# Routing attention with a tanh-shrink block: four pairs turned on TensorE, and the similarities turned and routed in PSUM between the fill's products

## The chip, the cores and the metric

The kernel runs on one core of one Trainium2 chip. A core has TensorE (matrix products, written to PSUM), VectorE, ScalarE and GpSimd (called DVE, ACT and POOL in the profile), the SyncE queue (SP) that issues most transfers here, and 16 DMA engines. The metric is device time in microseconds (us) of the whole program, the median of its runs; lower is better. The profile is of one further execution of the same program. A difference under 0.3% is about what the runs of this kernel can't tell from no difference.

## The reference

The program is attention in which a query attends only to the keys of its own cluster, followed by a two-layer block. `q`, `k` and `v` have 4 batches, 8 heads, 768 positions and 64 dimensions; each head has 16 centroids.

```python
q_assign = np.argmax(np.einsum('bhsd,hcd->bhsc', q_n, c_n), axis=-1)
k_assign = np.argmax(np.einsum('bhsd,hcd->bhsc', k_n, c_n), axis=-1)
mask = q_assign[:, :, :, None] == k_assign[:, :, None, :]
scores = scale * np.matmul(q, k.transpose(0, 1, 3, 2))
scores = np.where(mask, scores, -1000000000.0)
...
attn = np.exp(scores)
attn = attn / (np.sum(attn, axis=-1, keepdims=True) + 1e-09)
return np.matmul(attn, v).astype(np.float32)
...
h = x @ w_in
g = h - np.tanh(h)
return (g @ w_out).astype(np.float32)
```

`q_n`, `k_n` and `c_n` are the rows divided by their norms. Between the two parts the heads are put side by side, so `x` has 3072 rows of 512; `w_in` is 512 by 2048 and `w_out` 2048 by 512.

## The kernel before, in words

**Pairs and steps.** Two heads of one batch make a pair; there are 16, four a batch (`HP = 4`, `pairs` numbered 0 to 15). A pair's queries come in two halves of 384 columns, and its keys in three groups of two blocks of 128 (`NS = 3`). One *step* is a pair, a half and a group of keys: `steps` lists 96 of them. The first 12 (`HALF`) take pairs 0 to 3 with their first halves, the next 12 the same pairs' second halves, and from step 24 on each pair has six steps in a row (pair 4 has steps 24 to 29, and so on). In a step TensorE makes the scores of the *following* step (`begin`, L481), ScalarE their exponential (L503), VectorE multiplies it by the mask, which compares the codes of queries and keys (`select`, L513), and TensorE multiplies the step's own masked weights by `v` (`value`, L536). In the first halves of pairs 1 to 3 the mask is added to the scores on TensorE instead (L492), from one-hot codes (`hot`, prepared by VectorE in `one_hot`, L456 and L460, after a transfer that spreads the codes), and the sums of the weights are a product too (L551).

**The fill.** From step 12 on TensorE also computes the second block for the batch whose attention is finished. Its products are cut into items, and the loop over steps takes as many as its share of the work. Steps 12 to 23 do up-products L710 and down-products L726 of batch 0's first half; steps 24 to 47 the second half; from step 48 on each batch has 24 steps of seven-product (Strassen) items, first 56 short ones (L913, evacuated by L908 on VectorE and L918 on ScalarE, with the tanh L980 or L967), then 21 long ones (L1009). The last batch's come after the last step. A product takes a bank from the PSUM pool `ps_f`, which has three; the similarities, the codes on their way out (`pq`) and the denominators share them. The scores live in `ps_s`, two tiles of two banks.

**Where other work goes.** The order on every engine is the order in which the program issues. Each step collects a list `todo`: the two masks of the following step, the stages of pairs to come, sums, weights to be rounded, checks. `between`, which every product calls after its matmuls (most after their evacuation), spreads the list evenly over the step's products. In steps 24 to 35 the masks are taken ahead of the first product.

**From a pair to its codes.** `load` brings `q` and `k`, `turn` puts head dimensions on partitions, `similar` makes the products with the centroids (L376, 16 small ones on one `ps_f` bank), `turn_back` puts positions on partitions again (L386), `route` finds the largest of 16 (L394) and marks it (L396), `route_on` multiplies the marks by 16, 15, ..., 1 (L405) and takes the largest as the code (L407), `publish` turns the codes (L423) and sends them to DRAM (`q_codes`, L429). From there `spread` and `spread_both` bring them back to all partitions as `row` and `hot`.

Pairs 0 and 1 (`rowwise`) are loaded by rows, one transfer a head (L332), turned by six TensorE transposes into a `ps_s` tile (L355) and copied out by ScalarE or VectorE (L362, L364). All others are loaded as 32 by 32 blocks, two transfers a head (L340), and turned by one VectorE transpose per operand (L348). In the prologue, pairs 0 and 1 are taken through all stages by hand.

The dictionary `ready` places the stages of the other pairs. For pairs 2 and 3 the first step is 3 * (n - 2): turns at 0, `similar` at 1, `route` and `route_on` at 1, `publish` and the spreading at 2, `one_hot` at 4. For pairs 4 to 15 it is step 18 (pair 4) or the first step of the pair before: turns one step earlier, `similar` at 0, `route` at 1, `publish` at 3. A stage with two parts puts its second under `BEHIND + i`. In the loop over steps, stage 1 (`similar`) is taken ahead of `begin`, and where the step has a stage 1 and is past the first 12, `value` goes before both (`values_first`). `turn_back` then is the first entry of `todo`, ahead of the masks.

Of the kernel before, what the change touches and what calls it, by code (L numbers as in the profile page):

```python
# [30 lines left out]
F32 = mybir.dt.float32  # L31
# [8 lines left out]
P = 128  # L40
# [18 lines left out]
def kernel(  # L59
# [119 lines left out]
    def fast():  # L179
# [133 lines left out]
        def rowwise(n: int):  # L313

            return n < 2
# [66 lines left out]
        def turn_back(n: int):  # L382

            ps = sims[n]
            t = sims[n] = rtp.tile([P, TB], F32, name="simt")
            nc.vector.transpose(out=t, in_=ps.rearrange("p i j t -> p (i j t)"))  # L386

        def route(n: int):

            G = HCH * 8  # L390
            pr = sims.pop(n).rearrange("p (g c) -> p g c", c=C)
            shape = [P, G, C]
            mx = rtp.tile([P, G], F32, name="mx")
            nc.vector.reduce_max(out=mx, in_=pr, axis=AX.X)  # L394
            top = tops[n] = rtp.tile(shape, F32, name="top")
            nc.vector.tensor_tensor(  # L396
                out=top, in0=pr, in1=mx.unsqueeze(2).to_broadcast(shape), op=ALU.is_ge
            )
# [3 lines left out]
        def route_on(n: int):  # L402
            top = tops.pop(n)
            places = down.unsqueeze(1).to_broadcast([P, HCH * 8, C])
            nc.vector.tensor_tensor(out=top, in0=top, in1=places, op=ALU.mult)  # L405
            code = codes[n] = codep.tile([P, 2, NCH, 2], F32, name="code")
            nc.vector.reduce_max(out=code.rearrange("p i j h -> p (i j h)"), in_=top, axis=AX.X)  # L407
# [651 lines left out]
        def before(n: int):  # L1059


            def turns():
                turn(n, 1, nc.vector)
                if n >= HP:
                    load(n + 1)

            yield turns, lambda: turn(n, 0, nc.vector)
            yield lambda: similar(n), lambda: turn_back(n)
            yield lambda: (route(n), routed.append(n))
            yield lambda: publish(n)  # L1070
            if masked(n, 0):
                yield lambda: spread_both(n)
                yield lambda: one_hot(n)
# [3 lines left out]
        ready, routed = {}, []  # L1077
        BEHIND = 6
        for n in range(2, len(pairs)):
# [5 lines left out]
            for i, stage in enumerate(before(n)):  # L1085
                at = ready.setdefault(first_step + places[i], {})
                if i < 2:
                    stage, at[BEHIND + i] = stage
                at[i] = stage
# [104 lines left out]
        for at, (n, half, s) in enumerate(steps):  # L1194
# [43 lines left out]
            if summed(n, half):  # L1238
                sum_up(n, half, s)
# [30 lines left out]

            todo = [stages[BEHIND + 1]] if BEHIND + 1 in stages else []
            before_masks = len(todo)
# [5 lines left out]
            todo += [stages[i] for i in (0, BEHIND, 5, 3, 4, 2) if i in stages]  # L1278
            if 2 in stages:
                if at < 2 * HALF or at >= 3 * HALF:  # L1280
                    stage = todo.pop()
                    todo.append(lambda stage=stage: (stage(), route_on(routed.pop())))
                else:
                    todo.append(lambda: route_on(routed.pop()))
# [35 lines left out]
            if 2 * HALF <= at < 3 * HALF:  # L1320
                masks = before_masks + (3 if half == 1 and s == NS - 1 else 2)
                for it in todo[:masks]:
                    it()
                todo = todo[masks:]
            place = iter(range(slots))

            def between():
                i = next(place)
                for it in todo[i * len(todo) // slots : (i + 1) * len(todo) // slots]:
                    it()  # L1330

# [230 lines left out]
```

## Time and profile before

| what | before |
|---|---|
| median of 3 runs | 970.29 us (969.69 to 972.4) |
| the profiled execution, its own time | 971.36 us |
| its span, first to last instruction | 969.6 us |
| mean granted TensorE clock | 0.996 |
| TensorE busy | 940.6 us, 97% |
| VectorE busy | 599.9 us, 62% |
| GpSimd busy | 516.1 us, 53% |
| ScalarE busy | 290.0 us, 30% |
| DMA moved | 139.85 MB, 144 GB/s mean |

In the profile, L396 is line 396 of the kernel. A group's row reads: line, engine, operation, result and operands by the program's names, shapes, count; then busy us and mean ns of one; then the idle time of the engine just before them, with what ended it. In a timeline the first two numbers are the start and the length in us, and a bracket at the end holds the idle time of that engine just before, and its releaser. PE is TensorE's matmul stream; PEld its weight loads, which run beside it; SPq is SyncE's queue issuing a transfer. The chain of work that ended last is followed backwards from the last instruction, at each step to what released it.

### The profile page before, as it was taken

The numbers are of one execution on the slowest core, as the hardware profiler recorded it, in microseconds if no ns is written. First come the engines' busy times: TensorE is split into PE (matmuls) and PEld (weight loads), VectorE is DVE, ScalarE is ACT, GpSimd is POOL, SyncE is SP. The second block draws the span as 40 slices with busy tenths as digits, with TensorE's granted clock in tenths as the row PEclk, the third lists the DMA queues.
The fourth block names the chain that finished last, engine by engine and source line by source line (L and its number), as shares of the span: only waits on it lengthen the run. The fifth ranks groups of instructions, "written<-read, shape, count | busy, mean of one in ns | idle before, by whom it ended". The sixth has DMA issues, their size and how long they took to land.

```text
span 969.6 us, 16882 instructions
## 1 busy us (share of the span) xinstructions
PE 940.6 (97%) x6560; PEld 456.6 (47%) x6560; DVE 599.9 (62%) x1102; ACT 290.0 (30%) x449; POOL 516.1 (53%) x364
## 2 busy tenths in 40 slices
PE   8789999999999998999999999999999999999997
PEld 5333443345653333443455555444455555444664
DVE  7538588877767878767764558767664447443011
ACT  5366655224342232233221121333232211212000
POOL 1015344446666554787686344767788344566500
PEclk9989999999999999999999999999999999999999
DMA  9947445792654736464464747355454133223321
GB/s 199 192 133 157 153 132 144 226 275 91 167 140 144 187 106 149 151 151 147 158 183 149 203 134 207 112 156 140 135 160 145 66 107 103 88 103 130 105 104 36
DMA packets 181996, 139.85 MB, mean 144 GB/s; under 512 B 133604, under 2 KB 160660, under 8 KB 179220
## 3 DMA queue, kind: packets, MB, share of 16 engines
q1 hardware_dynamic: 175524, 117.15, 44.0%
q0 software_dynamic: 6240, 21.50, 6.9%
q8 instruction: 54, 0.88, 0.4%
q14 instruction: 34, 0.28, 0.1%
q10 hardware_dynamic: 144, 0.03, 0.0%
HBM read 117.48 MB, written 21.17 MB: 143 GB/s over the span
## 4 chain that ended last, share of the span: by engine, by line
PE 81%; DVE 10%; DMA 4%; SPq 2%; issue 2%; ACT 1%; POOL 0%; DVEq 0%; ACTq 0%; POOLq 0%
PE pd L1009 22%; PE pu L913 22%; PE sc L481 12%; PE av L536 11%; PE o L726 6%; PE h L710 4%; DVE e L513 3%; DVE t L348 1%; DMA row<-q_codes 1%; DVE top L396 1%; SPq L340 1%; PE sim L376 1%; DMA q_codes<-qc 1%; DVE top L405 1%; DMA stream<-up_factors 1%
## 5 line engine op out<-in xcount | busy, mean ns | idle before, releaser
L527 POOL TENSOR_TENSOR sum<-sum,e 128x768 f32<-128x768 f32 x112 | 211.1, 1884 | 89.3 <-DVE e L513 85.1
L513 DVE SCALAR_TENSOR_TENSOR e<-row,code,sc 128x384 f32<-128x384 bf16 x336 | 186.2, 607 | 62.9 <-ACT sc L503 59.2
L503 ACT ACTIVATE sc<-sc 128x768 f32<-128x768 f32 x168 | 125.8, 791 | 243.0 <-PE sc L481 233.7
L1009 PE MATMUL pd<-stream,G 128*64 128x256 f32 x1728 | 191.0, 379 | 0.0
L913 PE MATMUL pu<-xT,stream 128*64 128x384 f32 (+1 forms) x1024 | 158.6, 447 | 0.9 <-DMA stream<-up_factors 0.9
L1009 PEld LDWEIGHTS pd<-stream,G 128*64 128x64 f32 x1728 | 123.8, 137 | 67.0 <-issue 6.6
L481 PE MATMUL sc<-t,t 64*128 64x384 f32 x768 | 150.5, 510 | 0.3 <-ACT e L503 0.3
L536 PE MATMUL av<-e,vals 128*64 128x384 f32 x768 | 146.7, 501 | 1.3 <-DMA x<-in_k_dram 1.3
L982 POOL TENSOR_TENSOR G<-G,th 128x768 f32<-128x768 f32 (+1 forms) x51 | 87.2, 1722 | 88.5 <-ACT th L980 88.5
L913 PE MATMUL pu<-diff,stream 128*64 128x384 f32 (+1 forms) x768 | 121.1, 448 | 8.1 <-DVE G L908 2.9
L913 PEld LDWEIGHTS pu<-xT,stream 128*64 128x64 f32 x1024 | 72.5, 137 | 75.9 <-issue 61.9
L481 PEld LDWEIGHTS sc<-t,t 64*128 64x128 f32 x768 | 66.3, 187 | 72.0 <-issue 36.8
L536 PEld LDWEIGHTS av<-e,vals 128*64 128x64 f32 x768 | 48.1, 137 | 85.0 <-issue 79.3
L980 ACT ACTIVATE th<-G 128x768 f32<-128x768 f32 (+1 forms) x51 | 40.7, 805 | 152.4 <-DVE G L908 152.4
L726 PE MATMUL o<-w_out,g 128*64 128x512 f32 x384 | 86.0, 593 | 0.0
L913 PEld LDWEIGHTS pu<-diff,stream 128*64 128x64 f32 x768 | 53.7, 137 | 65.7 <-issue 44.9
L523 POOL TENSOR_TENSOR sum<-e 128x768 f32<-128x768 f32 x28 | 52.7, 1882 | 55.3 <-DVE e L513 34.5
L908 DVE TENSOR_TENSOR G<-pu,u 128x384 f32<-128x384 f32 x72 | 39.6, 550 | 34.1 <-PE pu L913 34.1
L1020 DVE SCALAR_TENSOR_TENSOR c<-pd,du 128x256 f32<-128x256 f32 x36 | 15.2, 421 | 68.0 <-PE pd L1009 68.0
L726 PEld LDWEIGHTS o<-w_out,g 128*64 128x64 f32 x384 | 27.2, 137 | 50.9 <-issue 49.7
L1020 DVE SCALAR_TENSOR_TENSOR du<-pd,du 128x256 f32<-128x256 f32 x27 | 11.4, 420 | 58.1 <-PE pd L1009 58.1
L710 PE MATMUL h<-xT,w_in 128*64 128x384 f32 x256 | 42.8, 486 | 0.0
(136 smaller groups left out, 848.0 us busy)
## 6 DMA issues: line engine op xcount, KB each, us to landing
stream<-up_factors SPq DMA_DIRECT2D x32, 896.0 KB
stream<-down_factors SPq DMA_DIRECT2D x21, 1024.0 KB
raw<-in_moe_w_in_dram POOLq DMA_DIRECT2D x16, 512.0 KB, 6.3
raw<-in_moe_w_out_dram POOLq DMA_DIRECT2D x16, 512.0 KB, 4.8
again<-in_moe_w_in_dram SPq DMA_DIRECT2D x32, 256.0 KB
again<-in_moe_w_out_dram SPq DMA_DIRECT2D x32, 256.0 KB
vals<-in_v_dram SPq DMA_DIRECT2D x32, 192.0 KB
row<-q_codes SPq DMA_DIRECT2D x29, 192.0 KB
```

Source lines behind the costliest of these rows:

```text
L481: nc.tensor.matmul(sc[i][:, h, 0:TB], lhsT=turned[n, 1][r].rearrange("p a n -> p (a n)")[:, j * P : (j + 1) * P], rhs=turned[n, 0][r, half ...
L503: nc.scalar.activation(out=out, in_=sc[i][:, :, 0:TB], func=ACT.Exp, scale=SCALE)
L513: nc.vector.scalar_tensor_tensor(out=e[:, h].rearrange("p (j n) -> p j n", n=P), in0=rows[n, half][:, :, h], scalar=codes[n][:, 1, j, h : ...
L523: nc.gpsimd.tensor_tensor(out=s, in0=pair[0], in1=pair[1], op=ALU.add)
L527: nc.gpsimd.tensor_tensor(out=s, in0=s, in1=pair[i], op=ALU.add)
L536: nc.tensor.matmul(avs[n, half][h * D : h * D + D], lhsT=vals[n][:, h, j], rhs=e[i][:, h], start=(j == 0), stop=(j == NCH - 1),)
L710: nc.tensor.matmul(h[r], lhsT=w_in[i][:, c, o * P : (o + 1) * P][:, r], rhs=xT[c][:, half], start=(c == 0), stop=(c == CD - 1),)
L726: nc.tensor.matmul(acc[sub][r], lhsT=gs[f % HF][:, f // HF, sub * P : (sub + 1) * P][:, r], rhs=w_out[f // FQ][:, f % FQ], start=(f == seq ...
L913: nc.tensor.matmul(ps[r], lhsT=streams[base + i][:, c, k_, r], rhs=right[c], start=(c == 0), stop=(c == CH - 1),)
L980: nc.scalar.activation(out=th, in_=t, func=ACT.Tanh)
L982: nc.gpsimd.tensor_tensor(out=t, in0=t, in1=th, op=ALU.subtract)
L1009: nc.tensor.matmul(ps[r], lhsT=left(i)[:, r], rhs=t[:, i], start=(i == 0), stop=(i == HF - 1))
```

## The change

1. `rowwise` holds for pairs 0 to 3. Pairs 2 and 3 are loaded by rows and turned on TensorE, both operands copied out by ScalarE. In steps 0 and 3 these turns are issued between the products with `v` (`value`) and the sums (`sum_up`).
2. `turn_back` writes over its own input, the `sim` bank in PSUM. `route` then takes the maximum, marks it in place and multiplies by the places, all from PSUM; only the last result (`top`) is in SBUF. `route_on` is left with the last maximum. This holds for all pairs, the two of the prologue too.
3. For pairs 4 to 15, `similar` moves from the head of a step to the following step's list, and is followed there by `turn_back`, `route` and `route_on`, each an entry of its own after the masks. With no stage 1 in these steps, `values_first` no longer applies. The turns stay on the step before, in the same order.
4. For pairs 2 and 3 `similar` keeps its place; `turn_back`, `route` and `route_on` are one entry at the end of the stages' part of the list.

```diff
         def rowwise(n: int):
-            return n < 2
+            return n < HP
...
             ps = sims[n]
-            t = sims[n] = rtp.tile([P, TB], F32, name="simt")
-            nc.vector.transpose(out=t, in_=ps.rearrange("p i j t -> p (i j t)"))
+            t = sims[n] = ps.rearrange("p i j t -> p (i j t)")
+            nc.vector.transpose(out=t, in_=t)
...
             nc.vector.reduce_max(out=mx, in_=pr, axis=AX.X)
+            nc.vector.tensor_tensor(
+                out=pr, in0=pr, in1=mx.unsqueeze(2).to_broadcast(shape), op=ALU.is_ge
+            )
+            places = down.unsqueeze(1).to_broadcast(shape)
             top = tops[n] = rtp.tile(shape, F32, name="top")
-            nc.vector.tensor_tensor(
-                out=top, in0=pr, in1=mx.unsqueeze(2).to_broadcast(shape), op=ALU.is_ge
-            )
+            nc.vector.tensor_tensor(out=top, in0=pr, in1=places, op=ALU.mult)
...
             top = tops.pop(n)
-            places = down.unsqueeze(1).to_broadcast([P, HCH * 8, C])
-            nc.vector.tensor_tensor(out=top, in0=top, in1=places, op=ALU.mult)
...
             def turns():
-                turn(n, 1, nc.vector)
+                turn(n, 1, nc.scalar)
+                if rowwise(n):
+                    turn(n, 0, nc.scalar)
                 if n >= HP:
                     load(n + 1)
-            yield turns, lambda: turn(n, 0, nc.vector)
-            yield lambda: similar(n), lambda: turn_back(n)
-            yield lambda: (route(n), routed.append(n))
+            yield turns
+            if n < HP:
+                yield lambda: similar(n)
+            else:
+                yield None
+            yield lambda: (turn_back(n), route(n), route_on(n))
...
-                if i < 2:
-                    stage, at[BEHIND + i] = stage
-                at[i] = stage
+                if stage:
+                    ready.setdefault(first_step + places[i], {})[i] = stage
+            if n >= HP:
+                if not rowwise(n):
+                    ready[first_step - 1][TURN_Q] = lambda n=n: turn(n, 0, nc.vector)
+                ready[first_step + 1][2] = [
+                    lambda n=n: similar(n), lambda n=n: turn_back(n), lambda n=n: route(n),
+                    lambda n=n: route_on(n),
+                ]
...
             if summed(n, half):
+                if 0 in stages:
+                    stages.pop(0)()
                 sum_up(n, half, s)
...
-            todo = [stages[BEHIND + 1]] if BEHIND + 1 in stages else []
-            before_masks = len(todo)
+            todo = []
...
-            todo += [stages[i] for i in (0, BEHIND, 5, 3, 4, 2) if i in stages]
-            if 2 in stages:
-                if at < 2 * HALF or at >= 3 * HALF:
-                    stage = todo.pop()
-                    todo.append(lambda stage=stage: (stage(), route_on(routed.pop())))
-                else:
-                    todo.append(lambda: route_on(routed.pop()))
+            if TURN_Q in stages:
+                todo += [stages[0], stages[TURN_Q]]
+            todo += [stages[i] for i in (5, 3, 4) if i in stages]
+            route_items = stages.get(2, [])
+            todo += route_items if isinstance(route_items, list) else [route_items]
...
-                masks = before_masks + (3 if half == 1 and s == NS - 1 else 2)
+                masks = 3 if half == 1 and s == NS - 1 else 2
...
+            turned_at = max(slots - 1 - now[-1][1], 0) if now else 0
...
+                if i == turned_at and 0 in stages and TURN_Q not in stages:
+                    stages[0]()
```

More of the change, by code (lines that the diff above doesn't have):

```diff
@@ L1073, in before @@
                 yield lambda: one_hot(n)
-        ready, routed = {}, []
-        BEHIND = 6
+        ready = {}
+        TURN_Q = 6
         for n in range(2, len(pairs)):
@@ L1085, in fast @@
             for i, stage in enumerate(before(n)):
-                at = ready.setdefault(first_step + places[i], {})
-                if i < 2:
-                    stage, at[BEHIND + i] = stage
-                at[i] = stage
+                if stage:
[7 more added lines that the diff above has]
+                ]
         asked = [
```

## The prediction

> **What bounds the kernel now.** I read the page first: engine shares, then the chain of work that ended last (TensorE 81% of it, VectorE 10%).
>
> ```profile
> PE 940.6 (97%) x6560; PEld 456.6 (47%) x6560; DVE 599.9 (62%) x1102; ACT 290.0 (30%) x449; POOL 516.1 (53%) x364
> ```
>
> TensorE is idle for only 29.0 us of the 969.6 us span, so a change pays only where TensorE waits. The table of ten-us stretches puts 12.7 us of that in the first 70 us and 5.8 us in the last ten; 10.5 us is scattered. TensorE's timeline gives each wait and what ended it (in brackets); those that this change can reach:
>
> ```profile
> 27.59 0.86 PE L376 MATMUL sim<-t,bd 128*32 128x192 f32 x16 [2.22 <-DVE t L348]
> 48.31 0.50 PE L492 MATMUL sc<-hot 64*128 64x384 bf16 x4 [2.58 <-DVE hot L460]
> 64.34 0.82 PE L492 MATMUL sc<-hot 64*128 64x384 bf16 x4 [3.53 <-DVE hot L460]
> ...
> 247.44 0.86 PE L376 MATMUL sim<-t,bd 128*32 128x192 f32 x16 [0.50 <-DVE t L348]
> 287.15 0.86 PE L376 MATMUL sim<-t,bd 128*32 128x192 f32 x16 [0.74 <-DVE t L348]
> 375.43 1.51 PE L913 MATMUL pu<-diff,stream 128*64 128x384 f32 x8 [2.61 <-DVE simt L386]
> 447.99 1.51 PE L913 MATMUL pu<-diff,stream 128*64 128x384 f32 x8 [0.94 <-DVE G L908]
> ```
>
> Ahead of the 447.99 wait, VectorE runs L394, L396 (1.70 us), L405 (2.06) and L407 in one go, and the evacuation L908 stands behind them. The view of the tile `top` (ns, minimum/median/maximum) shows that L396 and L405 need not cost that; the groups by shape give the nearest operation on PSUM and the two ways of turning a pair:
>
> ```profile
> L396 DVE TENSOR_TENSOR top<-simt,mx x16: 557/1283/1992, 11.6 to 724.6; 128x384 f32<-128x384 f32 x16
> L405 DVE TENSOR_TENSOR top<-top,down x16: 542/2045/2060, 12.2 to 726.4; 128x384 f32<-128x384 f32 x16
> ```
> ```profile
> L908 DVE TENSOR_TENSOR G<-pu,u 128x384 f32<-128x384 f32 x72 | 39.6, 550 | 34.1 <-PE pu L913 34.1
> L348 DVE STREAM_TRANSPOSE t<-x 128x768 f32<-128x768 f32 x28 | 26.1, 956 | 1.0 <-DMA x<-in_k_dram 1.0
> L386 DVE STREAM_TRANSPOSE simt<-sim 128x384 f32<-128x384 f32 x16 | 9.3, 580 | 9.4 <-PE sim L376 9.4
> L355 PE MATMUL pt<-ident,x 128*128 128x128 f32 x24 | 3.0, 273 | 0.0
> L362 ACT COPY t<-pt 128x768 f32<-128x768 f32 x3 | 2.3, 801 | 6.0 <-PE pt L355 6.0
> ```
>
> For the start, the timeline at 34 us shows pair 2's codes ready at 35.23 and their DMA issued only at 37.28, behind loads on SP's queue:
>
> ```profile
> 34.12 3.06 SPq L332 DMA_DIRECT2D vals<-in_v_dram  x4
> 34.95 0.28 DVE L427 CAST qc<-pq 24x128 bf16<-24x128 f32 x1 [0.98 <-PE pq L423]
> 37.28 0.45 SPq L429 DMA_DIRECT2D q_codes<-qc  x1
> ```
>
> **What the Trainium skill says.** "SBUF — State Buffer", section Who interferes with whom: a VectorE instruction with two SBUF inputs contends with a GpSimd one that reads SBUF; with at most one SBUF input it doesn't. The trace agrees: L396 and L405 have two and spread from 542 to 2060 ns, while L908, one input in PSUM, averages 550. "PSUM — Partial Sum Buffer", section PSUM bank collisions raise a hardware error: accesses of two engines to one bank and quadrant must be kept apart; so the `sim` bank is lost to the fill until VectorE's last read of it. "TensorE: Matmul & The Clock Gate", section What's actually happening: an idle window of about 3.4 us halves the clock. Here the 3.53 us wait is followed by a granted clock of 0.68 over 60 to 70 us; the 2.58 us wait is not.
>
> **The change, part by part** (step numbers are places in `steps`).
>
> *The routing in PSUM.* L396 and L405 each get one PSUM input. No row shows VectorE reading and writing one PSUM bank. Bounds: 0.55 us an operation (L908, L386), or twice that, should the read and the write take turns. I take 0.55: L908's reads and L386's reads of PSUM show no surcharge. It frees 16 x (1242 - 550 + 1431 - 550) ns = 25 us of VectorE; worth something only at the waits below.
>
> *Four pairs through TensorE.* Pairs 2 and 3 lose four L348 (3.8 us of VectorE) and gain 24 L355 (12 take 1.47 us on the timeline: 2.94 us of TensorE) and four L362 (3.2 us of ScalarE). Their loads become 8 DMAs, not 16, with half as many packets: the four L340 groups take 3.04, 2.81, 3.71 and 2.52 us of SP, the L332 pairs 1.04 to 1.98 (mean 1.55), so SP is 12.1 - 6.2 = 5.9 us less loaded before 35 us.
>
> I follow TensorE through the start:
> - The `row` DMA (18.05) stands behind pair 2's first load. Pair 0's codes were issued at 14.48 and the next such DMA took 2.74, so it can go at 17.2, and its transfer meets fewer packets. VectorE's masks start when VectorE is free, at 20.35, not 21.45: -1.1.
> - Values of step 0 end at 23.4; 12 transposes to 24.9; the second copy ends at about 25.75; `sim` of pair 2 at 25.85 instead of 27.59. Pair 2's codes reach L423 at 32.95, not 34.63: -1.7.
> - In step 3 the copies for pair 3 queue on ScalarE behind two exponentials and one L149/L150 pair (1.55 us), which stand ahead in program order. TensorE: transposes to about 37.95, sums to 38.7, then it waits for the second copy at 39.6. `sim` at 39.7 against 39.34: the gain is spent, +0.35.
> - Pair 2's codes now meet a free SP: issue at 33.7, not 37.28. The landing took 5.76 us; the stretch 30 to 40 us has the DMA engines over full (share 1.37), so I let only 2.5 of the 3.5 us survive: `hot` by about 45, and TensorE needs it at 45.9. The 2.75 us that the wait at 48.31 costs goes: -2.4 in all.
> - Pair 3's codes shift with TensorE and, the list DMA ahead of them being earlier, 0.7 more: L492 of 64.34 at about 61.2, **-3.1**. A wait of some 2.9 us stays. Whether the clock still drops I can't tell from waits of 2.58 (no) and 3.53 (yes); I count nothing, and keep 2.9 us (what the entries from 64.3 to 71.3 exceed those of the step before) for the lower end.
>
> From 70 us TensorE is saturated, so this shift is kept to the end.
>
> *The similarities, from the step's head to between products, one step later* (pairs 4 to 15; their `load` and turns stay on the step before, no DMA changes queue). `sim` and its turn no longer stand ahead of the scores, and values no longer go first. On TensorE: values to `sim` and scores to fill cost 0.10 + 0.20 us of switching now; the new order costs 0.10 + 0.20 + 0.05, and 0.10 for product to `sim`: +0.15 a pair, +1.8 us. Wait by wait:
> - 247.44 and 287.15 (excess over the row's steady pace 0.67 and 0.91): turns are a step old by then, -1.6; but see 210.
> - 375.43 (excess 2.84): the third product no longer needs the `sim` bank, only the difference L879 ending at 373.94; -1.4.
> - 391.66, 445.54, 617.74, 671.61 (excess 0.67, 1.16, 0.67, 1.16, in sum 3.7): VectorE's block of 4.5 to 5.3 us shrinks to 2.8. Against that the fill has two banks while `sim` is held. Replaying step 55: evacuation at 2.05, two masks to 4.4, evacuation to 4.95, turn to 5.5, so a product wanting a bank at 4.8 waits 0.25; about 0.3 each remains: -2.5.
> - Pair 6 (wait of 0.94 at 264.54): its tanh comes ahead of the routing; replayed, -0.5 beyond the above.
> - Pair 5: TensorE is held at 210.82 by a factor's DMA, so moving 0.8 us of `sim` behind that point is lost, and the third product's evacuation, its tanh and so the exponentials of step 27 come later (222.5, not 221.65): +0.9.
> - Moving `sim` of pair 5 out of 206.11 only lengthens the wait at 210.82: counted in the last.
>
> Late sum: 1.8 - 1.6 - 1.4 - 2.5 - 0.5 + 0.9 = -3.3; VectorE's 2.9 us less in step 19 may bring that factor 0.4 earlier: **-3.7**.
>
> Copies and SP cost nothing elsewhere; their cover is ScalarE's idle 70%. The hook at `turned_at` never fires, and `route` stays three operations in one item.
>
> Sum -3.1 - 3.7 = -6.8. The profiled execution took 971.36 us with its span of 969.6; minus 6.8 that is 964.6, and from the median 970.29 it is **963.5 us**.
>
> **The rivals.**
> - *Slower: the held bank.* `sim` holds one of three `ps_f` banks through turn, maximum, comparison and multiplication. On two banks, two products cover 2.58 us; an evacuation behind all four and the last reduction comes 0.58 + 1.67 + 0.55 + 0.55 = 3.35 late, and with a pair of masks (1.13) 4.5: 0.8 to 1.9, mean 1.3 us lost for each of six pairs in up-steps, 7.8 us, with none of today's waits shortened: -3.1 + 1.8 + 7.8 = +6.5, 976.8 us. It decides once in-place operations cost about 1.1 us. For it: VectorE is 90% busy in those stretches, and ScalarE's tanh, then the exponentials, queue behind late evacuations. Against: step 55's replay.
> - *No change: the codes' DMA is bound by traffic, not by SP.* Then 48.31 keeps its wait, step 3's copies cancel the rest: start 0, late -1.5: 968.8. For it: the full DMA engines. Against: half the packets of two pairs go.
> - *More: the clock never drops* and the factor comes early: another -4.5, 959.
>
> **How the numbers follow.** Chances: forecast 0.35 (own range 960.5 to 967.4), clock rival 0.13, no change 0.19, held bank 0.33. A difference under 0.3% (2.9 us) is about what a measurement of this kernel can't tell from none. Faster is 0.35 + 0.13 = 0.48; same 0.19; slower 0.33. The range runs from 957, some way into the clock rival, to 978, just above the held bank's 976.8, leaving out its worse half and the doubled price of in-place operations in every pair.
>
> **What would show it.** Right: L386 near 0.58 and the comparison and multiplication near 0.55 us with no spread; 48 L355; no wait at 48; no wait for L348 before `sim`. The held bank: new TensorE waits ended by L908 or by the routing within the step after `sim`, above 0.5 us, for pairs 5, 6, 9, 10, 13, 14. No change: q_codes issued at 34 but `hot` still landing near 47. Wrong altogether if in-place turns in PSUM take over 1.1 us, or if transposes wait for `ps_s`.

## The result, and the profile after

The changed kernel takes 966.11 us, median of 5 runs (965.49 to 966.62); the kernel before takes 970.65 us in the same comparison (5 runs, 969.69 to 972.4). The medians lie 4.5 us apart, where 6.8 were forecast. The ratio on record is 0.994, 95% interval 0.9917 to 0.9962, which is 3.7 to 8.1 us less; the quotient of the two medians, 0.9953, lies inside it. The profiled execution took 965.51 us with a span of 963.6 us; that of before had 971.36 and 969.6, so the two traces differ by 6.0 us.

First, the engine shares on the changed kernel's page:

```profile
PE 944.9 (98%) x6584; PEld 459.0 (48%) x6584; DVE 572.9 (59%) x1098; ACT 293.2 (30%) x453; POOL 511.4 (53%) x364
```

VectorE has 27.0 us less work, TensorE 4.3 us more, and TensorE's idle time went from 29.0 to 18.7 us. In the chain that ended last TensorE holds 92% (81% before) and VectorE 4% (10%).

The views of the tiles `mx`, `sim` and `top` of the changed kernel give minimum/median/maximum in ns, then the first and last start:

```profile
L386 DVE STREAM_TRANSPOSE sim<-sim x16: 583/595/599, 10.6 to 720.6; 128x384 f32<-128x384 f32 x16
L394 DVE TENSOR_REDUCE mx<-sim x16: 534/557/559, 11.2 to 721.2; 128x24 f32<-128x384 f32 x16
L395 DVE TENSOR_TENSOR sim<-sim,mx x16: 565/566/567, 11.8 to 721.8; 128x384 f32<-128x384 f32 x16
L400 DVE TENSOR_TENSOR top<-sim,down x16: 557/557/558, 12.4 to 722.4; 128x384 f32<-128x384 f32 x16
```

The turn, which now reads and writes the same PSUM bank, takes 15 ns more than the 580 of before, and the comparison takes 566 ns. The comparison and the multiplication, 557 to 1992 and 542 to 2060 ns before, have no spread left. In the trace of before, each of the 21 instructions of these two that took over 0.6 us ran while GpSimd was at work for at least 79% of its time, and the nine during which GpSimd did nothing took 557 to 559 ns. In the changed kernel GpSimd worked beside 16 of the 32 for three quarters of their time or more, and the times are 557 to 567 ns all the same.

TensorE's timeline of the changed kernel, at the waits of over 0.4 us between 30 and 450 us, with one of the shorter ones at the end:

```profile
40.02 0.86 PE L376 MATMUL sim<-t,bd 128*32 128x192 f32 x16 [0.45 <-ACT t L362]
63.31 0.82 PE L492 MATMUL sc<-hot 64*128 64x384 bf16 x4 [4.57 <-DVE hot L460]
...
209.46 1.52 PE L913 MATMUL pu<-xT,stream 128*64 128x192 f32 x16 [1.38 <-DMA stream<-up_factors]
223.99 0.87 PE L913 MATMUL pu<-diff,stream 128*64 128x192 f32 x8 [0.98 <-DVE t L908]
...
370.79 0.87 PE L913 MATMUL pu<-diff,stream 128*64 128x384 f32 x4 [1.04 <-DVE diff L879]
...
437.75 2.80 PE L913 MATMUL pu<-xT,stream 128*64 128x384 f32 x16 [0.21 <-PE pu L913]
```

The waits of 27.59, 48.31, 247.44 and 287.15 are gone or under 0.2 us, that of 375.43 is down from 2.61 to 1.04 with a further 0.30 at 373.25, and that of 447.99 (0.94) is gone. The wait for a factor's transfer (`stream`), 0.91 us at 210.82 before, is 1.38 us. The one at pair 3's gathered products (64.34 before) has become longer: 4.57 us, not 3.53. The first four products behind it take 0.82 us and not 0.50, as in the kernel before: the clock still drops there. The granted clock is 0.50 from 61.82 to 68.65 us, and in the kernel before from 63.67 to 70.50.

Where the 6.0 us went follows from the starts of each step's scores (L481) in the two traces, after minus before:

| up to step | difference, us | what came since the row above |
|---|---|---|
| 3 | -0.84 | the row DMA and step 0 |
| 5 | +0.68 | transposes and the wait for ScalarE's copy |
| 7 | -2.08 | pair 2's codes no longer waited for |
| 10 | -1.04 | pair 3's wait 1.04 longer |
| 12 | -1.44 | |
| 48 | -3.21 | pairs 4 to 8 routed |
| 72 | -4.95 | pairs 9 to 12 |
| 95 | -5.92 | pairs 13 to 15 |
| the end | -5.99 | |

So the start gave 1.4 us where 3.1 were forecast, and the rest 4.5 where 3.7 were.

### The profile page after: what moved, and what is told of

Its sections match the earlier page's. It is cut to its first block, busy times and chain, and to the rows that moved or that the text cites. A ratio compares the mean times of both kernels' runs of the same rounds, so it can differ in the third digit from the quotient of the medians.

```text
span 963.6 us, 16921 instructions
## 1 busy us (share of the span) xinstructions
PE 944.9 (98%) x6584; PEld 459.0 (48%) x6584; DVE 572.9 (59%) x1098; ACT 293.2 (30%) x453; POOL 511.4 (53%) x364
## 4 chain that ended last, share of the span: by engine, by line
PE 92%; DVE 4%; DMA 2%; issue 1%; ACT 1%; SPq 0%; DVEq 0%; ACTq 0%
PE pu L913 25%; PE pd L1009 23%; PE sc L481 14%; PE av L536 13%; PE o L726 8%; PE h L710 4%; DVE e L513 1%; PE sim L376 1%; DMA hot<-q_codes 1%; PE warm L302 1%; DMA stream<-up_factors 1%; PE den L597 1%; PE den L551 1%; PE den L570 1%; DVE diff L879 0%
## 5 line engine op out<-in xcount | busy, mean ns | idle before, releaser
L527 POOL TENSOR_TENSOR sum<-sum,e 128x768 f32<-128x768 f32 x112 | 207.5, 1852 | 86.9 <-DVE e L513 82.7
L913 PE MATMUL pu<-xT,stream 128*64 128x384 f32 (+1 forms) x1024 | 159.9, 447 | 2.3 <-DMA stream<-up_factors 1.4
L481 PE MATMUL sc<-t,t 64*128 64x384 f32 x768 | 150.0, 509 | 0.3 <-ACT e L503 0.3
L913 PE MATMUL pu<-diff,stream 128*64 128x384 f32 (+1 forms) x768 | 121.2, 448 | 2.4 <-DVE diff L879 1.0
L913 PEld LDWEIGHTS pu<-xT,stream 128*64 128x64 f32 x1024 | 72.8, 137 | 77.0 <-issue 61.9
L481 PEld LDWEIGHTS sc<-t,t 64*128 64x128 f32 x768 | 66.2, 186 | 73.7 <-issue 35.8
L913 PEld LDWEIGHTS pu<-diff,stream 128*64 128x64 f32 x768 | 53.9, 137 | 59.6 <-issue 45.4
L908 DVE TENSOR_TENSOR G<-pu,u 128x384 f32<-128x384 f32 x72 | 39.6, 550 | 31.5 <-PE pu L913 31.4
```

The lines of the kernel that those rows point to most:

```text
L481: nc.tensor.matmul(sc[i][:, h, 0:TB], lhsT=turned[n, 1][r].rearrange("p a n -> p (a n)")[:, j * P : (j + 1) * P], rhs=turned[n, 0][r, half ...
L527: nc.gpsimd.tensor_tensor(out=s, in0=s, in1=pair[i], op=ALU.add)
L913: nc.tensor.matmul(ps[r], lhsT=streams[base + i][:, c, k_, r], rhs=right[c], start=(c == 0), stop=(c == CH - 1),)
```

## The experiments

The kernel before ran again beside each group of experiments: 970.46 us beside the first four, 969.34 beside the next four, 969.98 beside the last four. Its single executions range over some 7 us there, so a time below is read with its ratio and interval, and a trace is read for its waits. The edits are shown in part, against the changed kernel.

### The parts alone

**The rows alone.** From the changed kernel, the routing and its order are put back as they were:

```diff
-            t = sims[n] = ps.rearrange("p i j t -> p (i j t)")
-            nc.vector.transpose(out=t, in_=t)
+            t = sims[n] = rtp.tile([P, TB], F32, name="simt")
+            nc.vector.transpose(out=t, in_=ps.rearrange("p i j t -> p (i j t)"))
...
-            yield lambda: (turn_back(n), route(n), route_on(n))
+            yield lambda: similar(n), lambda: turn_back(n)
+            yield lambda: (route(n), routed.append(n))
```

> The kernel before with one part of the change: pairs 2 and 3 loaded by rows, turned on TensorE and copied out by ScalarE between the products with v and the sums; routing and places as before. Theory (the parts add up): the whole start of the changed kernel is here and nothing late, so -1.4 us at step 12 and the same at the end, about 969.2 against 970.6; the wait of 2.6 us for the one-hot codes of pair 2 is gone and that for pair 3 is longer, 4 to 4.6 us. Rival (the start's gain needs the shorter routing too): within 0.5 us of before.

Measured: 970.93 us, ratio 1.0003 (0.9992 to 1.0013). Alone, the rows bring nothing that can be measured. Its TensorE timeline has the start of the changed kernel and the late waits of the kernel before:

```profile
63.55 0.82 PE L492 MATMUL sc<-hot 64*128 64x384 bf16 x4 [4.69 <-DVE hot L460]
...
247.12 0.86 PE L376 MATMUL sim<-t,bd 128*32 128x192 f32 x16 [0.50 <-DVE t L348]
...
286.74 0.86 PE L376 MATMUL sim<-t,bd 128*32 128x192 f32 x16 [0.74 <-DVE t L348]
375.01 2.17 PE L913 MATMUL pu<-diff,stream 128*64 128x384 f32 x8 [2.61 <-DVE simt L386]
```

At step 12 it was 1.4 us ahead of the kernel before. Of this 1.0 was lost by step 48; the last line shows the rest of the loss: after the same wait of 2.61 us the eight products took 2.17 us, where the trace of before has 1.51. The granted clock dropped here (0.81 from 372 to 378 us), and 1.7 us went. The wait at 375 us was thus dearer than its length: in some executions the clock drops behind it.

**Routing and order without the rows.** `rowwise` is left at two pairs, and the turns of pairs 2 and 3 go back to the step's list:

```diff
-            return n < HP
+            return n < 2
```

> The changed kernel with that part undone: pairs 2 and 3 are loaded as blocks and turned by VectorE after the masks. Theory: the start is as before (waits of 2.6 and 3.5 us for the one-hot codes), the late part keeps its -4.5 us: about 966.2. Rival (early and late overlap: what is won early is lost in a later wait for a transfer): the same as the changed kernel or better, 964 to 965.

Measured: 968.57 us, ratio 0.9976 (0.9963 to 0.9989), with single executions from 962.8 to 970.6. The trace, of an execution near the lower end (964.06 us), keeps its distance to the changed kernel from step 18 on within 0.9 us, and has at the start

```profile
28.20 0.86 PE L376 MATMUL sim<-t,bd 128*32 128x192 f32 x16 [2.22 <-DVE t L348]
48.65 0.82 PE L492 MATMUL sc<-hot 64*128 64x384 bf16 x4 [2.78 <-DVE hot L460]
```

and no wait at pair 3's codes at all: here the weight pieces, to which a section below comes, were requested 2.6 us after the transfer of these codes. The median is neither the 966.2 expected nor the rival's 964 to 965. This execution was 2.7 us behind the kernel before at step 7 and 2.9 us ahead of it at step 10. Which of pairs 2 and 3 waits, and whether the clock drops, thus goes with the landing of two transfers.

**The routing in SBUF, all else as changed.** Only the turn's target differs; comparison and multiplication then have SBUF operands again, in the new order:

```diff
-            t = sims[n] = ps.rearrange("p i j t -> p (i j t)")
-            nc.vector.transpose(out=t, in_=t)
+            t = sims[n] = rtp.tile([P, TB], F32, name="simt")
+            nc.vector.transpose(out=t, in_=ps.rearrange("p i j t -> p (i j t)"))
```

> The changed kernel, but the similarities are turned into an SBUF tile and routed there, at the same places between the products: the bank is free after the turn, and the comparison and the multiplication have two SBUF inputs again. Theory (contention with GpSimd is what the routing cost): they take 1.2 to 2 us where GpSimd is busy, 25 us of VectorE come back, and in the steps of short products TensorE waits 0.5 to 1.2 us again: +2 to +3.5 us over the changed kernel, about 969. Rival (the held bank costs): as fast as the changed kernel or up to 2 us faster, since the bank is held only for the turn.

Measured: 967.72 us, ratio 0.9972 (0.9958 to 0.9985). The tile views show the spread back:

```profile
L395 DVE TENSOR_TENSOR simt<-simt,mx x16: 557/559/1514, 12.0 to 725.0; 128x384 f32<-128x384 f32 x16
L400 DVE TENSOR_TENSOR top<-simt,down x16: 557/896/2604, 12.5 to 726.5; 128x384 f32<-128x384 f32 x16
```

VectorE has 13.8 us more work than in the changed kernel, not the 25 expected: 16 of these 32 operations, not nine as in the kernel before, met an idle GpSimd and took 557 to 559 ns. From step 48 to the end this trace keeps its distance to the changed kernel within 0.13 us, with the same waits. In the Strassen stretch it is the new order, with its single operations between products, that took the waits away; that the operations are in PSUM adds nothing there. The 3.2 us that it lost against the changed kernel came before step 48: 1.0 us by step 10, where pair 3's codes came later, 0.9 from step 12 to 18, 0.7 in pair 4's steps (L913 waits 1.64 us for L908 at 226.47, not 0.98), 0.7 in pair 5's. Only the last two, 1.3 us together, lie where the routing is at work. The intervals of this run and of the changed kernel's rerun below (0.9953 to 0.9974) overlap, so the time alone does not show what PSUM adds to the order.

**The routing in PSUM in the old order, without the rows.** `similar` stays at the head of a step and the turn and routing are whole, as before:

```diff
-            yield lambda: (turn_back(n), route(n), route_on(n))
+            yield lambda: similar(n), lambda: turn_back(n)
+            yield lambda: (route(n), routed.append(n))
```

> The kernel before, with the turn and the routing in PSUM but every stage at its old place, so for pairs 4 to 15 the bank is held from the head of one step into the list of the next, 7 to 10 us. Theory (two banks are enough most of the time): the comparison and the multiplication near 0.56 us, waits behind the routing shrink, about 1 us of new waits on the bank: 968 to 970. Rival (the held bank costs 1.3 us a pair in steps of short products, six pairs): +5 us or more over before, 975 to 978, with waits of TensorE for evacuations (L908 of before) in those steps.

Measured: 970.79 us, ratio 1.0006 (0.9991 to 1.0021). Here the held bank shows, in TensorE's timeline:

```profile
258.21 0.87 PE L913 MATMUL pu<-xT,stream 128*64 128x192 f32 x8 [0.74 <-DVE top L400]
...
442.46 1.51 PE L913 MATMUL pu<-xT,stream 128*64 128x384 f32 x8 [1.15 <-DVE top L400]
668.63 1.51 PE L913 MATMUL pu<-xT,stream 128*64 128x384 f32 x8 [1.15 <-DVE top L400]
```

A bank that waits from the head of one step for its routing in the next costs up to 1.15 us where a product needs it, and in this trace such waits take back a part of what the faster operations save (it ends 1.0 us ahead of the kernel before). Of 12 pairs the trace shows it at three. The operations in PSUM alone bring nothing that can be measured; the new order without them, in the run above, kept 0.9972.

### Is the bank or VectorE's queue the limit?

Three further maxima per pair from 4 on, 0.56 us each: once on the bank, ahead of the first comparison, and once on `top` behind the bank's release.

```diff
-            nc.vector.reduce_max(out=mx, in_=pr, axis=AX.X)
+            for _ in range(4 if n >= HP else 1):
+                nc.vector.reduce_max(out=mx, in_=pr, axis=AX.X)
```

> The changed kernel with three further maxima over the similarities in PSUM (0.56 us each, about 1.7 us in all) ahead of the first comparison, for pairs 4 to 15: the bank is held 1.7 us longer and VectorE has 20 us more work in all. To be read against the run beside it, which has the same work behind the bank's release. Theory (the bank's release lies beside other products wherever the step has fill work left): within 1 us of that run's total; no new wait over 0.5 us at the products that follow. Held-bank rival: 6 to 20 us above that run, with a wait of 0.5 to 1.7 us released by the routing (L400) in most pairs.

```diff
             nc.vector.tensor_tensor(out=top, in0=pr, in1=places, op=ALU.mult)
+            for _ in range(3 if n >= HP else 0):
+                nc.vector.reduce_max(out=mx, in_=top, axis=AX.X)
```

> The changed kernel with three further maxima over `top` in SBUF behind the product that releases the bank, for pairs 4 to 15: the same 20 us of VectorE work, the bank free as before. Theory: VectorE is idle 41% of the span, so no more than 2 us above the changed kernel. If it is more, VectorE's own queue is close to the end's path there, and the routing that the change made shorter counts for that reason too.

Measured: 972.71 us (ratio 1.0027, 1.0015 to 1.0039) with the bank held, 972.13 us (1.0017, 1.0004 to 1.0031) with it free. The two lie within 0.6 us, and in their traces the distance of each step is the same from step 42 on (0.67 us, to 0.84 at the end). The bank's holding time costs nothing, and the held-bank rival is out for the new order.

But both lost some 6 us against the changed kernel, where 2 at most were expected, for 17 to 18 us more of VectorE by their pages. Nearly all of it came before step 42. Against the changed kernel's trace, the run with the free bank lost 1.1 us from step 12 to 18, where none of the added work has run yet, 4.7 in pair 4's steps, 1.1 in pair 5's, and from step 42 to the end 0.15 us, though the greater part of the added work lies there. TensorE's timeline of this run where the 4.7 and the 1.1 of pair 5's steps went:

```profile
211.87 1.52 PE L915 MATMUL pu<-xT,stream 128*64 128x192 f32 x16 [2.26 <-DMA stream<-up_factors]
228.17 1.34 PE L915 MATMUL pu<-diff,stream 128*64 128x192 f32 x8 [2.74 <-DVE t L910]
269.15 0.87 PE L915 MATMUL pu<-diff,stream 128*64 128x192 f32 x8 [0.83 <-DVE t L910]
```

(L915 and L910 are the changed kernel's L913 and L908.) The wait of 0.98 us at 224 became 2.74, 1.76 more for 1.7 us of work; the eight products behind it took 1.34 and not 0.87 us, as the clock dropped (0.89 from 216 to 232 us); and the factor's wait, 1.38 us in the changed kernel, is 2.26 here, with a further 0.48 at 208.08. VectorE is idle 41% of the span, and in these two pairs none of that is to be had. This is the stretch where VectorE's time counts, and where the routing in SBUF lost its 1.3 us.

### Pair 3's codes: what sets their landing

The largest miss is the wait at 63.31. In SyncE's timeline of the kernel before, pair 3's codes leave (`q_codes`) and are spread as one-hot codes (`hot`) at

```profile
52.39 0.35 SPq L429 DMA_DIRECT2D q_codes<-qc  x1
55.46 1.28 SPq L445 DMA_DIRECT2D hot<-q_codes  x2
```

SyncE's and GpSimd's timelines of the changed kernel show both earlier, and two pieces of weights (`raw`, 512 KB each) that are requested around the second transfer:

```profile
50.52 0.35 SPq L429 DMA_DIRECT2D q_codes<-qc  x1
54.42 1.29 SPq L445 DMA_DIRECT2D hot<-q_codes  x2
```
```profile
54.01 0.53 POOL L218 DMA_DIRECT2D raw<-in_moe_w_in_dram  x1 [4.00 <-ACT rest L150]
55.33 0.53 POOL L218 DMA_DIRECT2D raw<-in_moe_w_in_dram  x1 [0.79 <-ACT rest L150]
```

The list `paces` says how many pieces a step requests. Five runs move them; nothing else differs from the kernel named. First the changed kernel once more, unedited:

> The changed kernel once more, unedited, so that the three runs that move weight pieces can be read beside it. Both theories: ratio to the kernel before 0.992 to 0.998, and in its profile the wait of about 4.5 us before pair 3's gathered products (L492, released by the one-hot codes L460) near 63 us. If this execution shows that wait shorter than 3 us, the wait itself varies from execution to execution, and the ledger of a single profile must be read with that.

Measured: 965.62 us, ratio 0.9963 (0.9953 to 0.9974); the wait before L492 is 4.72 us. From the first to the last step its trace stays within 0.6 us of the first one, so the wait is no accident of one execution.

```diff
-        paces = dict(enumerate((0, 0, 1, 1, 1, 0, 2, 1, 2, 1, 1, 0, 3, ...
+        paces = dict(enumerate((0, 0, 1, 1, 1, 0, 1, 2, 2, 1, 1, 0, 3, ...
```

> The changed kernel with one of the two weight pieces that step 6 requests (at 54.0 and 55.3 us, just ahead of pair 3's one-hot transfer at 54.4) requested a step later: the paces of steps 6 and 7 are 1 and 2 and not 2 and 1. Nothing of the computation changes. Theory (the weight pieces' traffic sets when pair 3's one-hot codes land): half of the traffic gone, the codes land about 1 us earlier, the wait before L492 goes from 4.57 to 3.6 us or less, the total 1 to 3 us below the changed kernel. Rival (latency and SyncE's order set it, and the pieces only share the time): the wait stays within 0.4 us of 4.57 and the total within 1 us of the changed kernel.

```diff
-        paces = dict(enumerate((0, 0, 1, 1, 1, 0, 2, 1, 2, 1, 1, 0, 3, ...
+        paces = dict(enumerate((0, 0, 1, 1, 1, 0, 0, 2, 2, 2, 2, 0, 3, ...
```

> The changed kernel with both of these weight pieces requested later: paces of steps 6 to 10 are 0, 2, 2, 2, 2 and not 2, 1, 2, 1, 1. Theory: the one-hot codes land 1.5 to 2.5 us earlier, the wait before L492 falls below 3 us and the drop of TensorE's clock behind it goes with it, so 3 to 7 us below the changed kernel, unless the pieces are then late for the first products that need them, which would show as a wait on them after 80 us. Rival: the wait stays within 0.4 us of 4.57, the total within 1 us.

```diff
-        paces = dict(enumerate((0, 0, 1, 1, 1, 0, 2, 1, 2, 1, 1, 0, 3, ...
+        paces = dict(enumerate((0, 0, 1, 1, 1, 1, 1, 1, 2, 1, 1, 0, 3, ...
```

> The changed kernel with one of these weight pieces requested a step earlier, in step 5, ahead of pair 3's list: paces of steps 5 to 7 are 1, 1, 1 and not 0, 2, 1. Theory: the traffic moves onto the landing of pair 3's codes and list (q_codes of 50.5 us), which then lands later, so the wait before L492 is as long or longer, 4.5 to 5.5 us, and the total is 0 to 2 us above the changed kernel. Rival: wait and total unchanged, within 0.4 and 1 us.

```diff
-        paces = dict(enumerate((0, 0, 1, 1, 1, 0, 2, 1, 2, 1, 1, 0, 3, ...
+        paces = dict(enumerate((0, 0, 1, 1, 2, 0, 0, 2, 2, 1, 1, 0, 3, ...
```

> The changed kernel with the two weight pieces of step 6 moved apart: one two steps earlier, one a step later (paces of steps 4 to 7 are 2, 0, 0, 2 and not 1, 0, 2, 1). Theory: as with both later, pair 3's one-hot transfer has the queues to itself and the wait before L492 falls to 1 to 2 us with no drop of the clock; as no step has three pieces more, the wait of 7 us that the run with both later showed at 76 us stays away: 957 to 961 us. Rival: the earlier piece delays pair 2's codes or the scores of step 4 by 1 us or more, and the total is 961 to 965 us.

And in the kernel before, the first of these edits:

> The kernel before (none of the change) with one weight piece of step 6 a step later, as in the run that took the changed kernel to 961.4 us. Theory: pair 3's wait there is caused by the same traffic whatever turns the rows, so its 3.53 us fall to 2 to 2.8 us, the clock does not drop, and the time falls by 2.5 to 4 us to 965.5 to 967 us; the change is then worth 4 to 6 us on equal terms, and of the 5 that were lacking at the start none is due to the rows themselves. Rival (the longer wait comes with the change alone): 969 to 970.5 us, and the change is worth 8 us or more on these terms.

Measured. "Landing" is from the issue of `hot` (L445) to the start of VectorE's L456, which waits for it; "pieces" are the requests between 1 us before that issue and the landing; "ratio" is to the kernel before.

| run | pieces, us | `hot` issued | landing, us | wait before L492 | time, us | ratio |
|---|---|---|---|---|---|---|
| changed | 54.01, 55.33 | 54.42 | 8.2 | 4.57 | 966.11 | 0.994 (0.9917 to 0.9962) |
| one later | 53.96 | 54.00 | 6.9 | 2.90 | 961.38 | 0.9924 (0.9901 to 0.9947) |
| one earlier | 54.30 | 55.26 | 6.7 | 3.64 | 964.16 | 0.9952 (0.9934 to 0.997) |
| both later | none | 55.21 | 4.5 | 1.12 | 969.61 | 1.0006 (0.9992 to 1.002) |
| one earlier, one later | none | 55.96 | 4.6 | 2.68 | 962.27 | 0.992 (0.9903 to 0.9937) |
| before | 56.10, 57.41 | 55.46 | 8.2 | 3.53 | 970.65 | 1 |
| before, one later | 56.00 | 55.22 | 8.2 | 3.41 | 969.95 | 0.9993 (0.9982 to 1.0004) |

In the changed kernel the theory holds: with none, one and two pieces the codes land in 4.5 or 4.6, 6.7 or 6.9, and 8.2 us (8.3 in the unedited rerun). The lines of the runs with one later, one earlier, both later and one each way, in this order, one timeline each:

```profile
61.58 0.50 PE L492 MATMUL sc<-hot 64*128 64x384 bf16 x4 [2.90 <-DVE hot L460]
```
```profile
62.66 0.83 PE L492 MATMUL sc<-hot 64*128 64x384 bf16 x4 [3.64 <-DVE hot L460]
```
```profile
60.40 0.50 PE L492 MATMUL sc<-hot 64*128 64x384 bf16 x4 [1.12 <-DVE hot L460]
...
83.82 2.93 PE L481 MATMUL sc<-t,t 64*128 64x384 f32 x8 [7.01 <-DVE e L513]
```
```profile
61.30 0.50 PE L492 MATMUL sc<-hot 64*128 64x384 bf16 x4 [2.68 <-DVE hot L460]
```

The second number tells the clock while these four products run: 0.50 us at 1.12, 2.68 and 2.90 us of wait, and 0.82 or more from 3.64 on. With one piece later the clock stays at 1.00 until TensorE has finished. That is why one piece moved (1.67 us of wait) brought 4 us by step 10: the drop went with it. With one piece earlier the drop lasts 3.4 us, where it lasts 6.8 in the changed kernel, and by step 10 the gain is some 1.5 us. With one piece each way the clock drops too, 1.1 us after the four products have begun: 0.50 from 62.44 to 65.86 us.

Four expectations failed. With one piece earlier I expected a longer wait; the piece was out of the way before the codes came (requested at 51.61), and the wait fell to 3.64. With both later the wait fell furthest, but the total came 4.0 us above the unedited rerun: the second line of that run shows a new wait of 7.01 us from 76.8 on. The timeline of VectorE has the reason:

```profile
79.98 0.43 DVE L158 TENSOR_SCALAR w_in<-raw 128x512 uint32<-128x512 uint32 x1 [3.62 <-DMA raw<-in_moe_w_in_dram]
...
82.55 2.18 DVE L513 SCALAR_TENSOR_TENSOR e<-row,code,sc 128x384 f32<-128x384 bf16 x4
```

The rounding of the last delayed piece stood ahead of the masks in program order and waited for its data. The delayed traffic came back as a head-of-line wait (a wait of all that stands behind one item in a queue), and the clock dropped with it: 0.50 from 80.67 to 87.50 us, and the scores' eight products took 2.93 us. With one piece each way this stayed away, but neither the short wait nor the steady clock that I had expected came: the one-hot codes were issued at 55.96, 1.5 us later than in the changed kernel, so the wait was 2.68 us, and the clock dropped. The total, 962.27 us, is the rival's.

The fourth is the kernel before: the same edit brought nothing (969.95 against 969.98 us), and its landing stayed at 8.2 us with one piece where the changed kernel's fell to 6.9. In the trace, the clock's drop at 64 us lasts 3.4 us and not 6.8, so this execution was 1.6 us ahead from step 12 to 48; then the clock dropped behind the wait at 374 us (0.50 from 374.50 to 377.91), and the lead was gone. The rival's numbers came true here too: with one piece later in both kernels the medians lie 8.6 us apart (ratios 0.9924 and 0.9993, each to the kernel before beside it).

What differs between the landings of 8.2 and 6.9 us is the order: in the kernel before the remaining piece is requested 0.8 us behind the codes' transfer, in the changed kernel 0.04 to 1.0 us ahead of it. The packets in the traces show what the order does. In the kernel before with one piece later, 728 of the 1536 packets of the codes start between 1.0 and 2.5 us after the issue; then the piece's packets come, and in the next 1.5 us only 153 more start. In the changed kernel with one piece later, the piece's packets come first, the codes' begin 2.9 us after the issue, and all of them start within the next 3 us. And in the run without the rows, where both pieces are requested 2.6 us behind or later, nearly all the codes' packets have started before the first of a piece's, and the landing is 4.8 us. No run reverses the order in one kernel.

## Why the prediction was right, and where it was off

The forecast change of -6.8 us lies inside the measured interval (-8.1 to -3.7), and 966.11 us inside the range that the forecast gave itself, 960.5 to 967.4. The parts fit less well than the total: the start brought 1.7 us too little and the rest 0.8 us too much, and that these partly cancel is luck.

- **Operations on the PSUM bank at 0.55 us: right.** 566 and 595 ns in place, 557 from PSUM to SBUF, and 27.0 us less of VectorE where 25 and 3.8 were worked out. The upper bound of twice that did not come true.
- **The start up to pair 2's codes: right within 1.4 us, and 0.3 at its end.** `sim` of pair 2 came at 26.74 (forecast 25.85), that of pair 3 at 40.02 behind ScalarE's copies (39.7), the codes were issued at 35.09 (33.7; the loads ahead took 3.64 us of SyncE), `hot` came at 45.07 ("about 45"), and the wait of 48.31 went. That decides against the rival of no change: the codes were issued 2.2 us earlier and `hot` came 2.5 earlier. How much of this is SyncE's queue and how much the halved packets of the loads, no run separates. The shift of 2.1 us at step 7 compares with the -2.4 forecast.
- **Pair 3's codes: the term that failed.** "The list DMA ahead of them being earlier, 0.7 more" should have given -3.1 and left a wait of some 2.9 us. The codes were issued 1.87 us earlier, the transfer of `hot` 1.04 us, and it took the same 8.2 us to land, so it arrived 1.0 us earlier where TensorE was 2.1 us earlier. The wait grew to 4.57 us. The term was -0.7 and measured +1.0: the list ahead brought no extra gain (1.87 is 0.2 less than TensorE's 2.1), and from the issue of the codes to that of `hot` went 3.90 us where it was 3.07, which is the other 0.8. Why that first, small transfer took longer stays open: the traces with rows for pairs 2 and 3 have 3.4 to 4.7 us there, those without 2.3 to 3.1. The weight pieces on GpSimd's queue, which the prediction had not looked at, explain why `hot` needs 8.2 us and not 4.5 in the changed kernel, and so why the wait is long; they do not explain why it grew.
- **The clock: counted at nothing, and so it was.** It dropped in both kernels. The 2.9 us kept for the lower end are of the right size: in the run with one piece later, a further edit, the wait is 2.90 us, the clock does not drop, and the time is 961.38 us, against 959 for the rival in which the clock never drops.
- **Switching between products: mis-sized.** +0.15 us for each of 12 pairs was counted, +1.8 in all. By the starts of the steps' scores, the pairs with no wait to lose (8, 11, 12, 15 when routed) moved by -0.15, -0.21, 0.0 and -0.21 us, so the term is zero or slightly negative.
- **The single late waits: right in kind, smaller in two places.** Pairs 6 and 7: -1.19 and -0.81 (forecast -1.02 and -0.76 with switching). The 375 us wait and the routing blocks of pairs 9, 10, 13 and 14: -2.3, where -3.3 was worked out. Pair 5: +0.23, where +0.65 was (the factor, forecast 0.4 earlier, was not). Together -4.5 against -3.7.
- **The held bank: out.** In the new order no wait on the bank exceeds 0.3 us, and 1.7 us more of holding moved the time by 0.6 us. Its mechanism exists where the routing comes a step after the products: 1.15 us at 442.46 and 668.63 in that run.

So 4.5 us measured against 6.8 forecast is a matter of one term at the start (1.7 us short), partly made up late (0.8), with the rest in the spread of executions: the two traces differ by 6.0 us, the medians by 4.5. How the gain divides between rows, order and PSUM is not settled. By the medians, the rows alone gave nothing, PSUM in the old order nothing, PSUM and order without the rows 1.9 us, rows and order without PSUM 2.7, and all together 3.7 to 4.5; which of pairs 2 and 3 waits at the start, and whether the clock drops, differs from run to run by as much.

**A version that beats both** is the changed kernel with one weight piece a step later: 961.38 us (6 runs, 960.45 to 963.69), 0.9924 of the kernel before.

## What to carry to other kernels

When TensorE is moved forward, list every transfer that it waits for next, and look at all queues that send traffic at that moment, not only at the queue which issues it; a wait that a faster front exposes can cost more than its length where the clock drops behind it. A busy share says nothing of a stretch: put a known amount of extra work on an engine and read from the trace where the time moves, as 17 us on VectorE cost some 6 us here, and of its trace's 7.1 us 5.8 lay in the steps of two pairs. For buffers in PSUM, keep what reads them close behind what fills them: held for 1.7 us longer the bank cost nothing that could be measured, held over a step it cost 0.74 to 1.15 us at three of 12 pairs.

## What the runs showed of the hardware

- On a 128x384 float tile in one PSUM bank, VectorE's turn in place takes 595 ns, the comparison in place 566, and the multiplication from PSUM to SBUF 557, with a spread of at most 16 ns, whether GpSimd is at work or not. With the tile in SBUF (the run that routes there), the comparison and the multiplication take 557 to 559 ns while GpSimd does nothing, and up to 1514 and 2604 ns while it works.
- TensorE's clock: in the traces, the granted clock falls to 0.50 for 3.4 or 6.8 us at a time while TensorE still has work to come. Every wait of 3.41 us or more (3.41 to 7.01, eleven traces) brought a drop, and none under 2.28 us did. Between these it went either way: 2.28, 2.61, 2.62, 2.68, 2.74 and 2.78 us dropped it, 2.54, 2.55, 2.58, 2.61, 2.62 and 2.90 us did not. The wait at 375 us is on both sides with the same 2.61 us, and after 2.68 us (one piece each way) the drop began 1.1 us after TensorE was back at work. One drop of 3.4 us cost 1.7 us where TensorE was busy throughout (the rows alone, at 375 us). The "TensorE: Matmul & The Clock Gate" page of the Trainium skill, section What's actually happening, puts the idle window at about 3.4 us; the longer waits here agree, and drops after 2.3 to 2.8 us say that the length of the last wait is not all. Among 62 executions of the kernel before, those with a mean granted clock of 0.992 took 973.3 us (median of 7), those with 0.998 took 968.5 (of 5): a good part of its spread goes with such drops.
- 1536 packets of 256 bytes (the one-hot codes of a pair, 384 KB) land in 4.5 to 4.6 us with no piece beside them, in 6.7 to 6.9 beside one of 512 KB (packets of 4096 bytes) requested up to 1.0 us ahead, in 8.2 beside one requested 0.8 us behind, and in 8.2 to 9.2 beside two.
